# A 96-row pass taken apart: 64 rows of one half beside 32 rows of the other

## The chip, the cores and the metric

The kernel runs on one core of a Trainium2 chip. The metric is device time in microseconds of one execution, as the median of several runs. The core has a matrix engine (TensorE, PE in the profile, with its weight loads as PEld), a vector engine (VectorE, DVE), a scalar engine (ScalarE, ACT), GpSimd (POOL) and SyncE (SP), which issues most DMA transfers. Each engine works through its own instructions in order; engines wait for each other by semaphores.

## The reference

Two branches over an input of 2048 tokens with 576 features are mixed by a gate per token:

```python
def _A_ref(x, w_r, w_i):
    X = jnp.fft.rfft2(x, axes=(-2, -1)) * (w_r + 1j * w_i)
    return jnp.fft.irfft2(X, s=(S, D), axes=(-2, -1))

def _B_ref(x, w_gate, w_up, w_down):          # w_gate, w_up: 576 x 4608, w_down: 4608 x 576
    h = _gelu(x @ w_gate) * (x @ w_up)
    return h @ w_down

g = _sigmoid((A_x * gate_w).sum(-1, keepdims=True))
return g * _A_ref(A_x, w_r, w_i) + (1 - g) * _B_ref(B_x, w_gate, w_up, w_down)
```

## The kernel before

The float32 operands are split in a high and a low part, and a product of two such operands is made of three TensorE passes: high times high, low times high, high times low. A *pass* here is one weight load with one matmul behind it.

The gate and up products (`x @ w_gate` and `x @ w_up`) take most of the passes. For most of the work they are computed by a scheme with seven products of half-sized blocks, as in Strassen's method, in place of eight. The class `Block` holds the weights' side. Its groups run over the token halves and over pairs of 128 hidden features, 34 groups in all; `products(b, k)` runs one group with the seven products named a11, a12, s2, s3, s1, a22 and s4 (n = 0 to 6). Each product is made for two halves s = 0 and 1 of 128 rows of output each (gate and up), and each half goes into a PSUM buffer of 128 x 512: `px` (two buffers, px0 and px1) and `pgu` (two buffers) take turns as `fore` and `acc`.

The contraction over a block of 288 features is two tiles of 128 rows and a rest of 32. For one half, `seven` issues six passes of 128 rows (L1324) and for the rest one pass of 96 rows (L1326): the three passes of high and low parts are stacked as 3 x 32 rows, so that one pass does them. The stacked rest of the weights is loaded into a slot by a DMA of SP (`tail` in `prep`, L1303, tensor `tails`), the stacked rest of the inputs is in `til` or `xtl`.

After products 0, 2 and 3 ScalarE copies each half's buffer (`copy`, L234): for n = 0 into the buffer of `acc` (`px<-pgu` or `pgu<-px`), for n = 2 and 3 into `xraw`. The buffers then go on being added to: product 1 adds to those of product 0, product 3 to those of product 2, product 5 to those of product 3. After products 4 and 6 VectorE adds the buffer to `xraw` (`add`, L1367). In the opening group (k = 0) the copies of products 0 and 2 are issued directly behind the seven passes, before anything else (`soon`).

Between the products stand steps of the down product (`down`, L927): twelve passes of 128 rows over 288 columns into the buffer `pdn`, copied out with a scale by ScalarE (L959, `stg`) and added in DRAM by a DMA of GpSimd (L940). An ordinary group has one such step behind each product and two behind the last; the opening group has none behind its first five.

The spectral branch (the Fourier transforms) runs beside this on VectorE, ScalarE and the DMA queues, with some passes on TensorE (L332). It is written as generators, and its place among the rest is set while the program is being built: each pass adds to a credit (`tick`), and at each `gap()` the branch issues work for as long as credit is left, which is capped at 2.0. `at(n, fn)` puts a function off by n gaps. `gap()` thus sets the order of instructions on every engine. Part of the branch's work are the column butterflies, with quarter turns on ScalarE (`turned`, L248 and L249) and additions on VectorE (L257, L262, L278), on tiles that DMAs bring from DRAM (`rows<-away`).

Of the kernel before, what the change touches and what calls it, by code (L numbers as in the profile page):

```python
# [15 lines left out]
P = 128  # L16
# [143 lines left out]
def _build(nc, tc, a):  # L160
    with ExitStack() as ctx:
# [3 lines left out]
        vec, act, pl, pe = nc.vector, nc.scalar, nc.gpsimd, nc.tensor  # L165
# [4 lines left out]
        def f(x):  # L170
            return x.bitcast(F32)
# [52 lines left out]
        def ps_x(c):  # L224
            return psum.tile([P, TB], F32, name=f"px{c}", tag=f"px{c}", bufs=1)
# [7 lines left out]
        def copy(o, i):  # L233
            act.activation(o, i, AF.Copy)  # L234
# [497 lines left out]
        def tick(us):  # L732
            credit[0] += rate[0] * us

        def at(n, fn):

            if n == 0:
                fn()
                return
            later.append((count[0] + n, fn))  # L740
            later.sort(key=lambda x: x[0])

        def gap():

            count[0] += 1
            while later and later[0][0] <= count[0]:
                later.pop(0)[1]()
            if aux:
                aux.pop(0)()
            credit[0] = min(credit[0], cap[0])  # L750
            if not gens:
                return
            while credit[0] > 0:
                try:
                    v = next(gens[0])
                except StopIteration:
                    gens.pop(0)
                    v = None
                if v is None:
                    while side and credit[0] > 0:  # L760
                        v = next(side[0], None)
                        if v is None:
                            break
                        credit[0] -= v
                    return
                credit[0] -= v
# [42 lines left out]
        def seq(key, *steps):  # L809

            q = todo[key] = [fn for _, fn in steps]
            for n, _ in steps:
                at(n, lambda: q and q.pop(0)())

        def due(key):
            q = todo.pop(key, [])
            while q:
                q.pop(0)()
# [86 lines left out]
        def split_h(g, hold, wants=(), soon=False):  # L905

            def high():
                hold.append(take(wants))
                copy(hold[0][:, 0], g)

            def low():
                vec.tensor_tensor(hold[0][:, 1], g, f(hold[0][:, 0]), ALU.subtract)
                credit[0] -= 0.7

            return ((1, high), (2, low)) if soon else ((3, high), (5, low))
# [93 lines left out]
        ops = {}  # L1009
# [216 lines left out]
        class Block:  # L1226
# [87 lines left out]
                c, d = (2, 4)  # L1314
                seq(("b", k, m), (lead, total), (lead + c, high), (lead + c, tail), (lead + d, rest_of))

            def seven(self, ps, k, m, x, s, first, soon=None):

                due(("b", k, m))
                w, (xh, xl, xt) = self.slot(k, m), ops[x]  # L1320
                for t in range(2):
                    hi, lo = (w[:, n + P * s:n + P * (s + 1)] for n in ((256, 0), (768, 1024))[t])
                    for q, (l, x) in enumerate(((hi, xh), (lo, xh), (hi, xl))):
                        pe.matmul(ps, l, x[:, t], start=first and t == 0 and q == 0, stop=False,  # L1324
                                  skip_group_check=True)
                pe.matmul(ps, w[0:96, 512 + P * s:512 + P * (s + 1)], xt[0:96], start=False, stop=True,  # L1326
                          skip_group_check=True)
                tick(7 * 0.2265)
                if soon:
                    soon()  # L1330
                gap()

        def products(b, k):

            p, i = b.groups[k]
            j = p * NT + 2 * i
            u, u3 = ([xraw[:, 2 * q + s] for s in range(2)] for q in range(2))
            made = {}
            opening, end, turn = k == 0, k == len(b.groups) - 1, (p, i) == (0, NBLK - 1)
            if 0 < k < len(PAIRS):  # L1340
                for q in range(2):
                    for n, fn in zip((1, 6, 7, 9, 10), tail_piece(2 * k + q)):
                        at(n + 11 * q, fn)

            def finish(name, x, o):
                g, v = x
                hold = made[name] = []

                def mult():
                    vec.tensor_tensor(o, o, v, ALU.mult)  # L1350
                    credit[0] -= 0.69

                def gelu():
                    act.activation(o, g, AF.Gelu_apprx_tanh)

                wants = dict(c21=extra[1:], c22=extra[:1]).get(name, base)
                if end and name in ("c21", "c12"):
                    gelu()
                    seq((name, k), (1, mult), *split_h(o, hold, wants, True))
                else:  # L1360
                    soon = 0 if end else 1
                    high, low = (fn for _, fn in split_h(o, hold, wants))
                    late = name in ("c22", "c12") and not end
                    seq((name, k), (1 + late, gelu), (2 + (soon if name != "c21" else 0) + late, mult), (4 + soon + late - end, high), (5 + 2 * soon + late, low))

            def add(o, v):
                vec.tensor_tensor(o, o, v, ALU.add)  # L1367
                credit[0] -= 0.69

            fore, acc = ([f() for f in fs] for fs in ((ps_gu, ps_gu), (lambda: ps_x(0), lambda: ps_x(1)))[::1 - 2 * (k % 2)])  # L1370
            downs = (0, 0, 0, 0, 0, 1, 1) if opening else (2, 2, 2, 2, 2, 0, 0) if end else (1, 1, 1, 1, 1, 1, 2)
            for n, (name, nd) in enumerate(zip(("a11", "a12", "s2", "s3", "s1", "a22", "s4"), downs)):
                m = n + 3
                b.prep(k + m // 7, m % 7)
                if n == 0 and k:
                    b.load_d(k)
                if n == 4:
                    w, x = dns[:, j % 4:j % 4 + 2], b.both
                    copy(w[:, :, 0], x)

                    def rest_of(w=w, x=x):
                        vec.tensor_tensor(w[:, :, 1], x, f(w[:, :, 0]), ALU.subtract)
                        credit[0] -= 1.35

                    seq(("dn", j), (5, rest_of))
                if n == 3 and opening:
                    b.more()
                if n == 0:
                    b.load(k + 1, "r11", "r21")
                elif n == 3:  # L1390
                    b.load(k + 1, "r22")
                elif n == 4:
                    b.load(k + 1, "r12")
                if n == 4:
                    fore = [ps_x(s) for s in range(2)] if k % 2 else [ps_gu() for _ in range(2)]
                ps = acc if n in (2, 3, 5) else fore
                for s in range(2):
                    soon = opening and n in (0, 2)
                    b.seven(ps[s], k, n, name, s, n in (0, 4), (lambda n=n, s=s: copy((acc, None, u)[n][s], ps[s])) if soon else None)
                    if n in (0, 2, 3) and not soon:  # L1400
                        copy((acc, None, u, u3)[n][s], ps[s])
                    elif n in (4, 6):
                        at(0 if end else 1, lambda x=(u3, u)[n // 2 - 2][s], y=ps[s]: add(x, y))
                if turn and n == 1:
                    ops["hold"] = True
                if turn:
                    assert ops["kept"]
                    at(2, lambda name=name: swap(name))
                if n in (1, 4, 5, 6):
                    finish(*{1: ("c11", fore, gl[0]), 4: ("c22", u3, u3[0]), 5: ("c21", acc, gl[1]), 6: ("c12", u, u[0])}[n])  # L1410
                for _ in range(nd):
                    if pend:
                        down(*pend.pop(0))
                if end and n == 5:
                    while gens:
                        credit[0] = 1.0
                        gap()
                    load_last(1)
            if turn:
                at(1, lambda: ops.pop("hold"))  # L1420
            due(("dn", j))
            for tb, names in ((1, ("c21", "c22")), (0, ("c11", "c12"))):
                d = (p, i, tb, tuple((j + q, made[names[q]], (names[q], k)) for q in range(2)))
                pend.extend((d, t) for t in range(4))
# [46 lines left out]
        ps = ps_gu()  # L1471
# [87 lines left out]
        b = Block()  # L1559
# [72 lines left out]
```

## Time and profile before

| | |
|---|---|
| median of the two timed runs | 1417.51 us (1417.21 to 1417.8) |
| profiled execution | 1420.83 us, span 1419.1 us |
| mean granted TensorE clock | 0.968 |
| PE busy | 1334.9 us (94%), 7210 passes |
| DVE, ACT, POOL busy | 80%, 59%, 19% |
| DMA, mean over the span | 186 GB/s |

The span runs from the first to the last instruction of the profiled execution; the rest of its time lies around it. Busy time of TensorE counts the records of matmuls, which overlap, and whose ends are modelled: what a pass costs is read from the distance between starts. A wait is put down to the engine and line that ended it.

### The profile page before, as it was taken

The numbers are of one execution on the slowest core, as the hardware profiler recorded it, in microseconds if no ns is written. First come the engines' busy times: TensorE is split into PE (matmuls) and PEld (weight loads), VectorE is DVE, ScalarE is ACT, GpSimd is POOL, SyncE is SP. The second block draws the span as 40 slices with busy tenths as digits, with TensorE's granted clock in tenths as the row PEclk, the third lists the DMA queues.
The fourth block names the chain that finished last, engine by engine and source line by source line (L and its number), as shares of the span: only waits on it lengthen the run. The fifth ranks groups of instructions, "written<-read, shape, count | busy, mean of one in ns | idle before, by whom it ended". The sixth has DMA issues, their size and how long they took to land.

```text
span 1419.1 us, 20623 instructions
## 1 busy us (share of the span) xinstructions
PE 1334.9 (94%) x7210; PEld 1172.4 (83%) x7210; DVE 1140.0 (80%) x1750; ACT 842.2 (59%) x1419; POOL 273.3 (19%) x339
## 2 busy tenths in 40 slices
PE   9989789899999998899995986899999999999998
PEld 7878678788888887788884875788888888888888
DVE  7788677887999877687685766776899996999964
ACT  6565544467565656776664765766655557556552
POOL 0011111121111211122220121221211114111141
PEclk9999899899999999999997998999999999999999
DMA  9658788798676799989993784787877779877798
GB/s 346 184 121 178 176 184 182 155 259 182 133 134 133 132 304 295 245 179 268 325 228 88 209 210 105 145 197 144 213 131 135 137 131 231 168 136 138 134 207 219
DMA packets 169895, 263.33 MB, mean 186 GB/s; under 512 B 18688, under 2 KB 83520, under 8 KB 168768
## 3 DMA queue, kind: packets, MB, share of 16 engines
q0 software_dynamic: 47424, 91.51, 41.8%
q1 hardware_dynamic: 121936, 170.07, 37.8%
q8 instruction: 56, 0.92, 0.3%
q14 instruction: 47, 0.39, 0.1%
q10 hardware_dynamic: 432, 0.44, 0.1%
HBM read 141.23 MB, written 123.08 MB: 186 GB/s over the span
## 4 chain that ended last, share of the span: by engine, by line
PE 53%; ACT 4%; DVE 3%; DMA 2%; issue 1%; SPq 0%; DVEq 0%; ACTq 0%
PE pdn L927 19%; PE px L1324 14%; PE pgu L1324 14%; PE pgu L1326 2%; PE px L1326 2%; PE pdn L332 1%; DMA gub<-wf 1%; DMA rows<-away 1%; ACT low L248 1%; ACT low L249 1%; DVE rows L262 1%; ACT stg L959 0%; DVE rows L257 0%; ACT tmp L234 0%; DMA slot<-tails 0%
## 5 line engine op out<-in xcount | busy, mean ns | idle before, releaser
L940 POOL DMA_DIRECT2D yd<-stg x264 | 228.1, 867 | 1064.1 <-ACT stg L959 1004.0
L959 ACT ACTIVATE stg<-pdn,omg 128x576 f32<-128x576 f32 x276 | 204.6, 742 | 376.2 <-PE pdn L927 237.9
L927 PE MATMUL pdn<-dn,hb 128*128 128x288 f32 x1356 | 203.7, 298 | 5.0 <-ACT stg L959 5.0
L927 PEld LDWEIGHTS pdn<-dn,hb 128*128 128x128 f32 x1356 | 195.4, 191 | 14.1 <-ACT stg L959 6.0
L1324 PE MATMUL pgu<-til,gub 128*128 128x512 f32 x516 | 138.2, 404 | 33.7 <-ACT xraw L234 33.7
L1324 PE MATMUL pgu<-xhi,gub 128*128 128x512 f32 x480 | 152.2, 399 | 5.4 <-ACT px L234 4.0
L1324 PEld LDWEIGHTS pgu<-til,gub 128*128 128x128 f32 x516 | 97.7, 195 | 53.9 <-ACT xraw L234 34.6
L927 PE MATMUL pdn<-dn,ext 128*128 128x288 f32 x816 | 132.8, 299 | 9.2 <-ACT rows L234 9.2
L927 PEld LDWEIGHTS pdn<-dn,ext 128*128 128x128 f32 x816 | 124.6, 192 | 19.6 <-ACT rows L234 9.7
L927 PE MATMUL pdn<-dn,gub 128*128 128x288 f32 x816 | 130.9, 296 | 0.0
L927 PEld LDWEIGHTS pdn<-dn,gub 128*128 128x128 f32 x816 | 117.0, 191 | 0.0
L1311 DVE TENSOR_TENSOR gub<-low,gub 128x512 fp32r<-128x512 f32 x151 | 103.4, 685 | 16.7 <-ACT gub L234 16.7
L234 ACT ACTIVATE gub<-low 128x512 fp32r<-128x512 f32 (+1 forms) x163 | 100.7, 620 | 23.9 <-DVE low L1297 17.3
L1324 PE MATMUL px<-xhi,gub 128*128 128x512 f32 x344 | 110.1, 402 | 4.3 <-ACT pgu L234 4.3
L1324 PE MATMUL px<-til,gub 128*128 128x512 f32 x396 | 104.4, 400 | 9.0 <-ACT xraw L234 9.0
L1324 PEld LDWEIGHTS pgu<-xhi,gub 128*128 128x128 f32 x480 | 87.8, 190 | 21.6 <-ACT px L234 4.4
L1324 PE MATMUL pgu<-xlo,gub 128*128 128x512 f32 x240 | 94.2, 393 | 0.0
L1324 PEld LDWEIGHTS px<-til,gub 128*128 128x128 f32 x396 | 74.2, 192 | 24.1 <-ACT xraw L234 9.2
L1324 PEld LDWEIGHTS px<-xhi,gub 128*128 128x128 f32 x344 | 63.6, 193 | 15.8 <-ACT pgu L234 4.5
L1367 DVE TENSOR_TENSOR xraw<-xraw,px 128x512 f32<-128x512 f32 x68 | 45.6, 684 | 35.6 <-PE px L1326 35.4
L927 PE MATMUL pdn<-dn,hx 128*128 128x288 f32 x444 | 70.3, 294 | 0.0
L1326 PE MATMUL pgu<-til,gub 96*128 96x512 f32 x172 | 68.5, 398 | 0.0
(300 smaller groups left out, 2741.1 us busy)
## 6 DMA issues: line engine op xcount, KB each, us to landing
yd<-stg POOLq DMA_DIRECT2D x264, 288.0 KB, 5.0
low<-ws SPq DMA_DIRECT2D x114, 256.0 KB, 4.9
gub<-wd SPq DMA_DIRECT2D x68, 288.0 KB, 4.7
gub<-tails SPq DMA_DIRECT2D x179, 96.0 KB, 3.9
tails<-wtb SPq DMA_DIRECT2D x92, 112.0 KB, 3.5
slot<-tails SPq DMA_DIRECT2D x59, 96.0 KB, 4.1
gub<-ws SPq DMA_DIRECT2D x22, 256.0 KB, 5.0
rows<-away SPq DMA_DIRECT2D x32, 145.0 KB, 6.0
```

Source lines behind the costliest of these rows:

```text
L234: act.activation(o, i, AF.Copy)
L248: act.activation(o[0:64], x[64:128], AF.Copy, scale=-s)
L249: act.activation(o[64:128], x[0:64], AF.Copy, scale=s)
L262: vec.tensor_tensor(o, p, q, op)
L332: pe.matmul(v[:, al, :NK], cc[d][2 * al + q], two(x)[:, al], start=n == 0, stop=n == 2)
L927: pe.matmul(ps[half], h[:, l, c], d[:, q, half * HD:(half + 1) * HD], start=part == 0 and n == 0, stop=part == 1 and n == 2)
L940: pl.dma_start(yd[u], o, accum_op=ALU.add)
L959: at(n, lambda: put(u, lambda o: act.activation(o.rearrange("p (c k) -> p c k", c=2), v[:, :, 0:HD], AF.Copy, scale=omg[:, u:u + 1]), i == 0))
L1311: vec.tensor_tensor(v[:, 0:5:4], x, f(v[:, 1:4:2]), ALU.subtract)
L1324: pe.matmul(ps, l, x[:, t], start=first and t == 0 and q == 0, stop=False, skip_group_check=True)
L1326: pe.matmul(ps, w[0:96, 512 + P * s:512 + P * (s + 1)], xt[0:96], start=False, stop=True, skip_group_check=True)
L1367: vec.tensor_tensor(o, o, v, ALU.add)
```

## The change

`seven` now issues only the six passes of 128 rows for a half, and then a gap. When both halves have had theirs, a new function, `rest_of_seven`, issues the rest for both: four passes, of 64 rows (rows 0 to 63) for one half and 32 rows (rows 64 to 95) for the other, and then the same with the halves exchanged. The operands, and where they lie, are as before. The copies and additions that follow a half now stand behind the rest of both halves, and the special place of the opening group's copies is gone.

```diff
-            def seven(self, ps, k, m, x, s, first, soon=None):
+            def seven(self, ps, k, m, x, s, first):
...
-                pe.matmul(ps, w[0:96, 512 + P * s:512 + P * (s + 1)], xt[0:96], start=False, stop=True,
-                          skip_group_check=True)
-                tick(7 * 0.2265)
-                if soon:
-                    soon()
+                tick(6 * 0.2265)
                 gap()
+
+            def rest_of_seven(self, ps, k, m, x):
+
+                w, xt = self.slot(k, m), ops[x][2]
+                for n in range(2):
+                    for s, (lo, hi) in ((n, (0, 64)), (1 - n, (64, 96))):
+                        pe.matmul(ps[s], w[lo:hi, 512 + P * s:512 + P * (s + 1)], xt[lo:hi], start=False, stop=lo == (64, 0)[s],
+                                  skip_group_check=True)
+                tick(2 * 0.2265)
...
                 for s in range(2):
-                    soon = opening and n in (0, 2)
-                    b.seven(ps[s], k, n, name, s, n in (0, 4), (lambda n=n, s=s: copy((acc, None, u)[n][s], ps[s])) if soon else None)
-                    if n in (0, 2, 3) and not soon:
+                    b.seven(ps[s], k, n, name, s, n in (0, 4))
+                b.rest_of_seven(ps, k, n, name)
+                for s in range(2):
+                    if n in (0, 2, 3):
                         copy((acc, None, u, u3)[n][s], ps[s])
```

On TensorE, the first product of the first ordinary group (k = 1) stood like this; px0 and px1 are the buffers of the two halves, slot holds the weights.

```order
L1324 MATMUL px0_1027<-xhi0_63,slot_74 128x512 x2
L1324 MATMUL px0_1027<-xlo0_65,slot_74 128x512
L1324 MATMUL px0_1027<-xhi0_63,slot_74 128x512 x2
L1324 MATMUL px0_1027<-xlo0_65,slot_74 128x512
L1326 MATMUL px0_1027<-til0_302,slot_74 128x512
L1324 MATMUL px1_1028<-xhi0_63,slot_74 128x512 x2
L1324 MATMUL px1_1028<-xlo0_65,slot_74 128x512
L1324 MATMUL px1_1028<-xhi0_63,slot_74 128x512 x2
L1324 MATMUL px1_1028<-xlo0_65,slot_74 128x512
L1326 MATMUL px1_1028<-til0_302,slot_74 128x512
L927 MATMUL pdn_1062<-dn_75,hb2_79 128x288 x6
```

The same product in the changed kernel, in which the sizes are those of what is written:

```order
L1324 MATMUL px0_1041<-xhi0_63,slot_74 128x512 x2
L1324 MATMUL px0_1041<-xlo0_65,slot_74 128x512
L1324 MATMUL px0_1041<-xhi0_63,slot_74 128x512 x2
L1324 MATMUL px0_1041<-xlo0_65,slot_74 128x512
L1324 MATMUL px1_1042<-xhi0_63,slot_74 128x512 x2
L1324 MATMUL px1_1042<-xlo0_65,slot_74 128x512
L1324 MATMUL px1_1042<-xhi0_63,slot_74 128x512 x2
L1324 MATMUL px1_1042<-xlo0_65,slot_74 128x512
L1334 MATMUL px0_1041<-til0_302,slot_74 128x512
L1334 MATMUL px1_1042<-til0_302,slot_74 128x512 x2
L1334 MATMUL px0_1041<-til0_302,slot_74 128x512
L927 MATMUL pdn_1078<-dn_75,hb2_79 128x288 x6
```

The pass of half 0 that stood at L1326 between the halves is gone from there; four passes at L1334 stand behind both halves, ahead of the down step.

The second place is on ScalarE, where the profile of before has TensorE's longest wait, around 748 us. The first rows before, with the copy of half 0 (`xraw_83<-pgu_6432`) and the first of the branch's quarter turns:

```order
L234 ACTIVATE gub0_812<-pdn_6512 128x290
L234 ACTIVATE xraw_83<-pgu_6432 128x512
L234 ACTIVATE gub1_72<-low_76 128x2x256
L248 ACTIVATE low_76<-rows_94 64x580
L249 ACTIVATE low_76<-rows_94 64x580
```

Five such rows further on, the end of the branch's part, with the copy of half 1 (`xraw_83<-pgu_6433`) and the copy of a down step (L959) behind it:

```order
L249 ACTIVATE low_76<-rows_94 64x580
L234 ACTIVATE tmp_5046<-rows_94 128x580
L248 ACTIVATE wtb_88<-wtb_88 64x580
L249 ACTIVATE wtb_88<-wtb_88 64x580
L234 ACTIVATE xraw_83<-pgu_6433 128x512
L959 ACTIVATE stg0_84<-pdn_6595,omg_92 128x576
```

The same place in the changed kernel:

```order
L234 ACTIVATE gub0_812<-pdn_6771 128x290
L234 ACTIVATE gub1_72<-low_76 128x2x256
L234 ACTIVATE xraw_83<-pgu_6667 128x512
L234 ACTIVATE xraw_83<-pgu_6668 128x512
L959 ACTIVATE stg0_84<-pdn_6809,omg_92 128x576
L248 ACTIVATE low_76<-rows_94 64x580
L249 ACTIVATE low_76<-rows_94 64x580
```

Both halves' copies and the down step's copy now stand ahead of the branch's quarter turns. At the second longest wait, around 849 us, the order changes in the same way.

## The prediction

> **What bounds the kernel now.** I read the page first: the busy time of the engines, the slices, and the chain that ended last.
>
> ```profile
> span 1419.1 us, 20623 instructions
> PE 1334.9 (94%) x7210; PEld 1172.4 (83%) x7210; DVE 1140.0 (80%) x1750; ACT 842.2 (59%) x1419; POOL 273.3 (19%) x339
> ...
> PE   9989789899999998899995986899999999999998
> ...
> PE 53%; ACT 4%; DVE 3%; DMA 2%; issue 1%; SPq 0%; DVEq 0%; ACTq 0%
> ```
>
> TensorE is busy in 94% of the span and carries over half of the chain; no other engine has more than 4% of it. So a pass that takes longer on TensorE lengthens the kernel by as much, and what can be won beside that is the idle 84 us (1419.1 - 1334.9). Next I asked whom TensorE waited for, and what it did around the two longest waits; the columns of the second view are the stretch, its length, the busy time of each engine, and the granted clock.
>
> ```profile
> PE pgu L1324 <- ACT xraw L234: 33.7, 3, 15.8
> PE px L1324 <- ACT xraw L234: 17.1, 2, 9.0
> ...
> 740.00:764.00 24.00, 8.33 (x48) 7.08 (x46) 12.15 (x18) 11.73 (x20) 1.44 (x2) 0.75 0.47 116
> 764.00:779.50 15.50, 15.41 (x73) 13.56 (x74) 9.29 (x15) 6.89 (x12) 0.00 (x0) 0.83 0.36 112
> 848.00:863.00 15.00, 2.01 (x14) 1.70 (x12) 8.81 (x12) 8.08 (x13) 0.00 (x0) 0.72 0.30 67
> 863.00:878.50 15.50, 15.40 (x67) 13.01 (x68) 8.35 (x13) 8.02 (x14) 2.56 (x3) 0.83 0.56 107
> ```
>
> The idle time stands in a few lumps. The two largest leave TensorE idle for 24.00 - 8.33 = 15.7 us and 15.00 - 2.01 = 13.0 us, and after each the clock granted over the next 15.5 us is only 0.83. Both are waits for a ScalarE copy out of PSUM. They return below, because the change moves those copies.
>
> **The passes: what one costs.** The row counts the passes of 96 rows, and the timeline shows one among its neighbours (start, duration; PEld is the weight load that goes with each pass).
>
> ```profile
> 0.00:1419.10 1419.10, 188.64 (x476) 90.73 (x476) 0.97 0.80 186
> ...
> 300.55 0.19 PEld L1326 LDWEIGHTS px<-til,slot 96*128 96x128 f32 x1
> 300.77 0.39 PE L1326 MATMUL px<-til,slot 96*128 96x512 f32 x1
> 300.77 0.95 PEld L927 LDWEIGHTS pdn<-dn,ext 128*128 128x128 f32 x6
> 301.00 0.96 PE L927 MATMUL pdn<-dn,ext 128*128 128x288 f32 x6
> 301.67 0.85 PEld L927 LDWEIGHTS pdn<-dn,gub 128*128 128x128 f32 x6
> 301.80 0.95 PE L927 MATMUL pdn<-dn,gub 128*128 128x288 f32 x6
> 302.45 0.32 PEld L1324 LDWEIGHTS pgu<-xhi,gub 128*128 128x128 f32 x2
> 302.58 0.63 PE L1324 MATMUL pgu<-xhi,gub 128*128 128x512 f32 x2
> ```
>
> There are 476 such passes, two per product, so 238 products. A pass over 512 columns occupies TensorE for 301.00 - 300.77 = 0.23 us, though its record lasts 0.39: the next pass starts before the last one has drained. Passes over 288 columns follow at (301.80 - 301.00)/6 = 0.133 us. A weight load starts at the same moment as the pass ahead of it (300.77 and 300.77), and in no pass of the trace before it: loads run one pass ahead and no further. And a pass starts as little as 0.133 us after its own load did, so that this is the closest step at which the trace shows different weights taking their turn.
>
> The change takes out two passes of 0.23 us per product and puts in four: 64 rows for half 0, 32 rows for half 1, 64 rows for half 1, 32 rows for half 0. Streamed columns stay at 512 each. No short pass, and no two passes beside each other, stand in this trace, so the price per product is bounded:
>
> - From below, each 32-row pass lies wholly beside its 64-row pass: two steps of 0.23, extra 0. Less than that isn't to be had, since each half still needs rows 0 to 63 for one whole pass.
> - In between, passes on different rows run together but their weights come one after the other, as the loads above do. With the first short pass at 0, the second starts at 0.133; the third needs rows 0 to 63, free at 0.23, and its weights, at 0.267; the fourth starts at 0.40 (its rows are free at 0.363). The next full pass needs all rows: 0.40 + 0.23 = 0.63. Before it started at 0.46. Extra 0.17.
> - Strictly one after the other: 4 x 0.23 - 0.46 = 0.46 extra.
> - From above, each change of height lets the array drain, so that a pass is paid with its 0.39 and the full pass ahead with its last 0.16: 4 x 0.39 + 0.16 - 0.46 = 1.26 extra.
>
> I take the middle one, 0.17, since it is the only one that keeps both things the rows show, loads one ahead and a closest step of 0.133. Times 238: **+40.5 us**, with ends 0 and 300.
>
> Here a rule of the Trainium skill speaks for the lower end. The page "TensorE: Matmul & The Clock Gate", section "Part 3: Packing small matmuls — row/col tiling", says that matmuls on different row groups start some 4 ns apart; by it the sum of the passes would be an estimate of 238 x 2 x 0.004 = 2 us. The same section says that a weight load overlaps a running matmul only where the row group differs, which this trace contradicts: the loads at 300.77 and 301.00 run under passes on the same rows.
>
> **The copies.** After products 0, 2 and 3 of a group ScalarE copies each half out of PSUM, and the product that next adds to that buffer waits for it. Half 0 used to be copied under the seven passes of half 1; now both copies come behind the last short pass.
>
> ```profile
> 85.28 0.40 PE L1326 MATMUL pgu<-til,gub 96*128 96x512 f32 x1
> ...
> 85.71 0.58 ACT L234 ACTIVATE px<-pgu 128x512 f32<-128x512 f32 x1
> ...
> ACT xraw L234 <- PE pgu L1326: 20.3, 40, 1.4
> ACT xraw L234 <- PE px L1326: 19.3, 37, 2.2
> ```
>
> From the start of the last pass to the end of its copy is 85.71 + 0.58 - 85.28 = 1.0 us. In ordinary groups a down step of twelve passes, 12 x 0.133 = 1.6 us, lies between, and ScalarE stood waiting for the pass before 77 of 136 such copies: hidden, at nothing. If ScalarE were late by its usual other work (0.6 to 0.7 us) it would still nearly fit; without that cover 66 places would pay up to 1.0 - 0.23 = 0.8 us, 50 us in all. Only the opening group has no down step there: two places, 2 x 0.8 = **+1.6 us**. The loads of the tail weights on SP's queue wait for the last reader of a slot, which stands at the product's end as before; the loads behind it move only with TensorE.
>
> **The two long waits.** In program order ScalarE's copy stood behind quarter turns (L248) of the spectral branch's column butterflies, whose inputs a DMA brought late. Rows of ScalarE at both places:
>
> ```profile
> 750.10 0.69 ACT L248 ACTIVATE low<-rows 64x580 f32<-64x580 f32 x1 [4.74 <-DMA rows<-away]
> ...
> 763.44 0.60 ACT L234 ACTIVATE xraw<-pgu 128x512 f32<-128x512 f32 x1
> ...
> 849.14 0.69 ACT L248 ACTIVATE low<-rows 64x580 f32<-64x580 f32 x1 [2.69 <-DMA rows<-away]
> ...
> 862.45 0.60 ACT L234 ACTIVATE xraw<-pgu 128x512 f32<-128x512 f32 x1
> ```
>
> The order of the change has the branch some steps later at these places, and both halves' copies (and a copy for the down steps) ahead of the butterflies. TensorE can then do up to two more products and down steps, 8 to 10 us of passes, before the next copy behind the butterflies stops it: up to 18 us less in the two. Against it, where the branch's work is issued in the second gap of a product, both copies now stand behind it, which begins a wait one half earlier, 1.6 us; ten waits for such copies would make 16. What is late next is in the first case the copies of product 3, behind the same butterflies. I take **-8 us**, the larger of the two waits halved, out of -18 to +16.
>
> **The sum.** 40.5 + 1.6 - 8 = +34 us. The profiled execution took 1420.8 us with its span of 1419.1, which gives 1455; it stands 3.3 us above the median of the runs, 1417.5, so the forecast for the timed runs is **1452 us**, +2.4%.
>
> **Rivals.**
> 1. *The passes lie wholly beside each other*: 1417.5 + 1.6 - 8 = 1411. For it speaks that nothing but the weights joins the two rows' work; against it, that no load in the trace runs more than one pass ahead, though full passes can't show whether it might.
> 2. *The change doesn't do what it says*, and the four run one after the other: 238 x 0.46 = 110, so 1417.5 + 110 + 1.6 - 8 = 1521. For it: no two of 7210 passes run together in the trace, as none could.
> 3. *Drained only going in and out*: 0.16, then 0.23 for the first pair and 0.39 for the second, less 0.46, is 0.32; times 238 is 76, so 1487. Drained at every change of height: 300, so 1711. The trace has no change of height to speak for or against. A rule of the Trainium skill gives the last: "TensorEngine Tiling (Array Packing)", section "Tiling Modes", says that a change of tiling mode drains the engine, and 128, 64 and 32 rows are three modes there; no run here shows it yet.
> 4. *Faster*: the reordered copies free TensorE of both long waits while the passes cost nothing. Idle 15.7 + 13.0 us and two times 15.5 x (1 - 0.83) = 2.6 us at a reduced clock are 34 us: 1417.5 + 1.6 - 34 = 1385. It decides from the point where the copies of product 3 as well stand ahead of the butterflies; in the order they don't.
>
> **How the numbers follow.** Forecast 0.30, beside each other 0.29, one after the other 0.14, drained in and out 0.13, drained each time 0.07, faster 0.06, anything else 0.01. About 2%, 28 us, is what a measurement of this kernel can tell from no change, so same is 1389 to 1446. To it go rival 1 (0.29), a third of the forecast's own chance, whose range of 1435 to 1475 reaches below 1446 (0.10), and the rest (0.01): 0.40. Faster is rival 4, a little of which ends short: 0.05. Slower: 0.55. The range runs from 1398, rival 1 with most of the waits' gain, to 1530, rival 2 with the copies' waits unchanged; it leaves out rival 4 and the full drain, and fringes of the others, under 0.2. The likeliest case alone spans 1435 to 1475.
>
> **What would show it.** In the timeline of the changed kernel, the start of the second short pass after the first: near 0 for rival 1, 0.13 for the forecast, 0.23 or more for rival 2; and from the first short pass to the next full one 0.46, 0.63 or 0.92. The waits of TensorE for the copies at 748 and 850 us should have about halved in sum, and the opening group should show two waits under 1 us. The prediction is wrong if short passes cost by their rows instead of their columns, or if the branch, moved, meets its transfers at other places and makes new waits of ten microseconds.

## The result, and the profile after

The changed kernel takes 1691.04 us as the median of its runs (1688.97 to 1693.11) against 1417.51 us before: a ratio of 1.193, with a 95% interval of 1.1866 to 1.1993. The profiled execution has a span of 1691.0 us, 271.9 us more than before.

The page of the changed kernel, its span, the busy times, TensorE's slices and the chain that ended last:

```profile
span 1691.0 us, 21572 instructions
PE 1657.1 (98%) x7686; PEld 1224.8 (72%) x7686; DVE 1146.6 (68%) x1750; ACT 835.7 (49%) x1419; POOL 273.4 (16%) x339
PE   9999999999999999999997999999999999999999
PE 91%; ACT 3%; DMA 2%; DVE 2%; issue 1%; SPq 1%; DVEq 0%; ACTq 0%
PE pdn L927 27%; PE pgu L1324 18%; PE px L1324 18%; PE px L1334 11%; PE pgu L1334 11%; PE pdn L332 1%; DMA slot<-tails 1%; SPq L1221 1%; ACT stg L959 0%; PE px L863 0%; ACT low L248 0%; ACT low L249 0%; PE pgu L863 0%; DMA tmp<-xs 0%; DVE rows L262 0%
```

TensorE is now busy in 98% of a longer span, and 22% of that span is the new line, L1334, alone. The waits of TensorE in the changed kernel are fewer than before (engine and line, what it waited for, us in total, times, longest):

```profile
PE pgu L1324 <- ACT xraw L234: 13.7, 2, 10.4
PE pdn L927 <- ACT stg L959: 5.5, 4, 2.2
PE pdn L332 <- ACT stg L959: 4.3, 5, 0.9
PE px L1324 <- ACT xraw L234: 1.7, 2, 1.0
```

So the time went into passes, and some came back from waits. One product's rest in the timeline, weight loads first and then the passes:

```profile
1167.43 0.19 PEld L1324 LDWEIGHTS pgu<-xhi,gub 128*128 128x128 f32 x1
1167.66 0.19 PEld L1324 LDWEIGHTS pgu<-xlo,gub 128*128 128x128 f32 x1
1168.20 0.18 PEld L1334 LDWEIGHTS pgu<-xtl,gub 64*128 64x128 f32 x1 [0.35 <-issue]
1168.63 0.18 PEld L1334 LDWEIGHTS pgu<-xtl,gub 32*128 32x128 f32 x1 [0.25 <-issue]
1169.06 0.18 PEld L1334 LDWEIGHTS pgu<-xtl,gub 64*128 64x128 f32 x1 [0.25 <-issue]
1169.49 0.18 PEld L1334 LDWEIGHTS pgu<-xtl,gub 32*128 32x128 f32 x1 [0.25 <-issue]
1169.91 0.19 PEld L927 LDWEIGHTS pdn<-dn,hb 128*128 128x128 f32 x1 [0.24 <-issue]
```

```profile
1167.88 0.39 PE L1324 MATMUL pgu<-xlo,gub 128*128 128x512 f32 x1
1168.20 1.78 PE L1334 MATMUL pgu<-xtl,gub 64*128 64x512 f32 x4
1169.91 1.06 PE L927 MATMUL pdn<-dn,hb 128*128 128x288 f32 x6
1170.81 0.95 PE L927 MATMUL pdn<-dn,hx 128*128 128x288 f32 x6
```

Before, each load started with the pass ahead of it. Here the last full pass starts at 1167.88, and the first short pass's load only at 1168.20, together with its own pass; the next three loads follow at steps of 0.43 us, each with its pass, and so does the load of the next full pass at 1169.91. Here no pass runs beside another, and no weights are loaded ahead. From 1167.88 to 1169.91 are 2.03 us, where two passes of 96 rows took 3 x 0.23 = 0.69 from the last full pass to the next. One more 0.105 us follows: the six down passes from 1169.91 to 1170.81 take 0.90 us in place of 0.80. Together 1.34 + 0.105 = 1.445 us a product, and 238 products make 344 us. The span grew by 272. Of the other 72 us, 50 came back as idle time of TensorE, which fell from 1419.1 - 1334.9 = 84 us to 1691.0 - 1657.1 = 34. The rest is a remainder that wasn't measured by itself; it goes with the mean granted clock, which rose from 0.968 to 0.992, since the long waits were followed by stretches at a lower clock. Below, *waits* means both.

### The profile page after: what moved, and what is told of

Read it like the earlier page. It is cut to its first block, busy times and chain, and to the rows that moved or that the text cites. A ratio compares the mean times of both kernels' runs of the same rounds, so it can differ in the third digit from the quotient of the medians.

```text
span 1691.0 us, 21572 instructions
## 1 busy us (share of the span) xinstructions
PE 1657.1 (98%) x7686; PEld 1224.8 (72%) x7686; DVE 1146.6 (68%) x1750; ACT 835.7 (49%) x1419; POOL 273.4 (16%) x339
## 4 chain that ended last, share of the span: by engine, by line
PE 91%; ACT 3%; DMA 2%; DVE 2%; issue 1%; SPq 1%; DVEq 0%; ACTq 0%
PE pdn L927 27%; PE pgu L1324 18%; PE px L1324 18%; PE px L1334 11%; PE pgu L1334 11%; PE pdn L332 1%; DMA slot<-tails 1%; SPq L1221 1%; ACT stg L959 0%; PE px L863 0%; ACT low L248 0%; ACT low L249 0%; PE pgu L863 0%; DMA tmp<-xs 0%; DVE rows L262 0%
## 5 line engine op out<-in xcount | busy, mean ns | idle before, releaser
L959 ACT ACTIVATE stg<-pdn,omg 128x576 f32<-128x576 f32 x276 | 205.0, 743 | 550.9 <-PE pdn L927 291.4
L927 PE MATMUL pdn<-dn,hb 128*128 128x288 f32 x1356 | 213.3, 305 | 6.7 <-ACT stg L959 5.5
L927 PEld LDWEIGHTS pdn<-dn,hb 128*128 128x128 f32 x1356 | 186.2, 190 | 32.8 <-issue 23.4
L1324 PE MATMUL pgu<-xhi,gub 128*128 128x512 f32 x480 | 153.5, 402 | 14.8 <-ACT xraw L234 13.7
L1334 PE MATMUL pgu<-til,gub 64*128 64x512 f32 x344 | 153.6, 499 | 0.0
L927 PE MATMUL pdn<-dn,ext 128*128 128x288 f32 x816 | 143.7, 311 | 0.0
L927 PEld LDWEIGHTS pdn<-dn,ext 128*128 128x128 f32 x816 | 112.6, 188 | 31.3 <-issue 28.2
L1334 PEld LDWEIGHTS pgu<-til,gub 64*128 64x128 f32 x344 | 62.8, 182 | 95.0 <-issue 93.6
L1324 PE MATMUL pgu<-til,gub 128*128 128x512 f32 x516 | 125.4, 391 | 0.0
L1334 PE MATMUL px<-til,gub 64*128 64x512 f32 (+1 forms) x268 | 119.2, 497 | 0.0
L1311 DVE TENSOR_TENSOR gub<-low,gub 128x512 fp32r<-128x512 f32 x151 | 103.3, 684 | 13.7 <-ACT gub L234 13.7
L1334 PEld LDWEIGHTS px<-til,gub 64*128 64x128 f32 (+1 forms) x268 | 48.7, 182 | 72.4 <-issue 70.5
L1372 DVE TENSOR_TENSOR xraw<-xraw,pgu 128x512 f32<-128x512 f32 x68 | 43.7, 684 | 78.5 <-PE pgu L1334 78.5
```

The lines of the kernel that those rows point to most:

```text
L927: pe.matmul(ps[half], h[:, l, c], d[:, q, half * HD:(half + 1) * HD], start=part == 0 and n == 0, stop=part == 1 and n == 2)
L959: at(n, lambda: put(u, lambda o: act.activation(o.rearrange("p (c k) -> p c k", c=2), v[:, :, 0:HD], AF.Copy, scale=omg[:, u:u + 1]), i == 0))
L1311: vec.tensor_tensor(v[:, 0:5:4], x, f(v[:, 1:4:2]), ALU.subtract)
L1334: pe.matmul(ps[s], w[lo:hi, 512 + P * s:512 + P * (s + 1)], xt[lo:hi], start=False, stop=lo == (64, 0)[s], skip_group_check=True)
```

## The experiments

Two theories were put up after this result. **H**: a change of height (the 128, 64 or 32 rows of the array that a pass uses) makes TensorE empty itself first, and passes of one height on different rows do run beside each other. **S**: a short pass never runs beside another nor takes its weights ahead, whatever its neighbour.

**Short passes in order of height.** The four passes of the change, in another order:

```diff
-                for n in range(2):
-                    for s, (lo, hi) in ((n, (0, 64)), (1 - n, (64, 96))):
+                for lo, hi in ((0, 64), (64, 96)):
+                    for s in range(2):
```

> The four short passes of a product are put in order of height: 64 rows for half 0, 64 rows for half 1, then 32 and 32. Theory H (each change of height lets the array drain): one step of 0.32 us in, then 0.23 between the two of 64 rows, 0.43 to the first of 32, 0.23 between these, 0.42 out: 1.63 us from the last full pass to the next one in place of 2.03, so 238 x 0.40 = 95 us less than the change, some 1596 to 1610 us. Theory S (a short pass never takes its weights ahead, whatever its neighbour): 2.03 as before, 1691 us.

Measured: 1608.95 us, ratio to before 1.1362 (1.1342 to 1.1382), 82 us less than the change, as H has it. Its timeline, loads and passes:

```profile
1129.35 0.29 PEld L1334 LDWEIGHTS px<-til,gub 64*128 64x128 f32 x2 [0.35 <-issue]
1130.01 0.29 PEld L1334 LDWEIGHTS px<-til,gub 32*128 32x128 f32 x2 [0.36 <-issue]
1130.66 0.30 PEld L927 LDWEIGHTS pdn<-dn,hb 128*128 128x128 f32 x2 [0.36 <-issue]
```

```profile
1129.03 0.39 PE L1324 MATMUL px<-xlo,gub 128*128 128x512 f32 x1
1129.35 1.39 PE L1334 MATMUL px<-til,gub 64*128 64x512 f32 x4
1130.67 0.40 PE L927 MATMUL pdn<-dn,hb 128*128 128x288 f32 x1
```

The two loads of 64 rows now stand in one record of 0.29 us (0.18 for one): the second starts under the first pass, 0.11 us after it. From 1129.03 to 1130.67 are 1.64 us, against 1.63 forecast from H. S is out: a short pass takes its weights ahead when the pass in front has its own height.

**Two pairs of 64 rows.** The heights agree, and the halves lie on different rows:

```diff
+                xh = ops[x][0]
                 for n in range(2):
-                    for s, (lo, hi) in ((n, (0, 64)), (1 - n, (64, 96))):
-                        pe.matmul(ps[s], w[lo:hi, 512 + P * s:512 + P * (s + 1)], xt[lo:hi], ...
+                    pe.matmul(ps[0], w[0:64, 512 + P * n:512 + P * (n + 1)], xt[0:64], ...
+                    pe.matmul(ps[1], w[64:128, 256 + P * n:256 + P * (n + 1)], xh[64:128, 0], ...
```

> Four short passes per product as in the change, but all of 64 rows: rows 0 to 63 into the buffer of half 0 beside rows 64 to 127 into that of half 1, twice. It computes other sums (the lower rows are taken from other weights), only its time counts. Theory H: the two of a pair run beside each other, since their heights agree: 0.32 in, about 0 in the pair, 0.23, about 0, 0.42 out, 0.97 us from full pass to full pass in place of 2.03; 238 x 1.06 = 252 us less than the change, 1440 us, up to 1485 where the waits for ScalarE that the slower passes hid come back. If equal heights run without a drain but one after the other: 0.32 + 3 x 0.23 + 0.42 = 1.43, about 1550 us. Theory S: 1691 us.

Measured: 1495.37 us, ratio 1.0555 (1.0536 to 1.0575). Loads and passes of one product:

```profile
1043.36 0.18 PEld L1334 LDWEIGHTS px<-til,slot 64*128 64x128 f32 x1 [0.35 <-issue]
1043.36 0.18 PEld L1336 LDWEIGHTS px<-xhi,slot 64*128 64x128 f32 x1
1043.47 0.19 PEld L1334 LDWEIGHTS px<-til,slot 64*128 64x128 f32 x1
1043.47 0.19 PEld L1336 LDWEIGHTS px<-xhi,slot 64*128 64x128 f32 x1
1044.02 0.30 PEld L927 LDWEIGHTS pdn<-dn,ext 128*128 128x128 f32 x2 [0.36 <-issue]
```

```profile
1043.04 0.39 PE L1324 MATMUL px<-xlo,slot 128*128 128x512 f32 x1
1043.36 0.49 PE L1334 MATMUL px<-til,slot 64*128 64x512 f32 x1
1043.36 0.49 PE L1336 MATMUL px<-xhi,slot 64*128 64x512 f32 x1
1043.69 0.39 PE L1334 MATMUL px<-til,slot 64*128 64x512 f32 x1
1043.70 0.39 PE L1336 MATMUL px<-xhi,slot 64*128 64x512 f32 x1
1044.02 0.40 PE L927 MATMUL pdn<-dn,ext 128*128 128x288 f32 x1
```

The passes of a pair start within 0.01 us of each other, and their loads too. This is what the change was meant to get, and it got it nowhere. Two terms can be read off. Going from 128 rows to 64 takes 1043.36 - 1043.04 = 0.32 us instead of 0.23: 0.09 more, which fits an array that empties first (the emptying has no row of its own). And the first pass after a change of height starts together with its load, so that the next load begins 0.11 us later, and the next pass 1043.69 - 1043.36 = 0.33 us later instead of 0.23: 0.10 more. A change of height thus costs **some 0.2 us**, and a visit to another height two of them. From full pass to full pass it took 1044.02 - 1043.04 = 0.98 us, as expected (0.97), though the steps fall otherwise than I had them. The time was above my 1440 to 1485 because more waits came back than the 45 us allowed for: TensorE was idle for 1490.7 - 1422.4 = 68 us, 34 more than in the change, and the mean granted clock was 0.980, against 0.992.

**Two pairs of 32 rows** at the change's own places in the array:

```diff
-                    for s, (lo, hi) in ((n, (0, 64)), (1 - n, (64, 96))):
-                        pe.matmul(ps[s], w[lo:hi, 512 + P * s:512 + P * (s + 1)], xt[lo:hi], ...
+                    for s, lo in ((0, 0), (1, 64)):
+                        pe.matmul(ps[s], w[lo:lo + 32, 512 + P * n:512 + P * (n + 1)], xt[lo:lo + 32], ...
```

> Four short passes at the change's places in the array (rows from 0 for half 0, rows from 64 for half 1), but all of 32 rows, so that the heights agree. It leaves out the other rows of the rest. If unequal heights are what keeps the change's passes apart, pairs run beside each other as with two times 64 rows: 1495 us. If a pass of 32 rows can't run beside another, 0.23 to 0.43 us a pass and 1560 to 1691 us.

Measured: 1491.09 us, ratio 1.0527 (1.0498 to 1.0555), as with 64 rows. The four passes of one product stand in one record:

```profile
1042.71 0.73 PE L1334 MATMUL px<-til,slot 32*128 32x512 f32 x4
```

It lasts as long as the two pairs of 64 rows did, from 1043.36 to 1043.70 + 0.39. So neither the place nor 32 rows as such keeps the change's passes apart, only that their heights differ.

**One pair of 64 rows.** The second pair is left out:

```diff
-                for n in range(2):
...
+                xh = ops[x][0]
+                pe.matmul(ps[0], w[0:64, 512:512 + P], xt[0:64], ...
+                pe.matmul(ps[1], w[64:128, 256 + P:256 + 2 * P], xh[64:128, 0], ...
```

> One pair of 64 rows per product (rows 0 to 63 for half 0, rows 64 to 127 for half 1), in place of two pairs; it leaves out half of the rest and takes other rows for half 1. If a visit to another height costs a fixed price in and out, this is the run with two pairs less one step of 0.33 us: 1495 - 238 x 0.33 = 1416, up to 1440 as waits come back. If the price hangs on each short pass, half of what two pairs added to the move alone: 1431.6 + 32 = 1464.

Measured: 1457.95 us, ratio 1.0291 (1.0261 to 1.0322): 37 us less than two pairs, between the two expectations. My first one took away a step of 0.33 us, but 0.10 of that belongs to the visit and stays: 238 x 0.23 = 55, less what the waits take back. Even one pair, which has half the streaming time of two passes of 96 rows, is slower than these, at 1431.59 us in the same place (the move alone, below): what it saves, 0.23 us, is less than a visit's two changes.

**Four passes at full height.** As many passes as in the change, without a change of height:

```diff
-                    for s, (lo, hi) in ((n, (0, 64)), (1 - n, (64, 96))):
-                        pe.matmul(ps[s], w[lo:hi, 512 + P * s:512 + P * (s + 1)], xt[lo:hi], ...
+                    for s in (n, 1 - n):
+                        pe.matmul(ps[s], w[0:96, 512 + P * s:512 + P * (s + 1)], xt[0:96], ...
```

> Four passes per product as in the change, but each of 96 rows, which the program places at full height (128): halves 0, 1, 1, 0. The rest is thus added twice; only the time counts. If the changes of height are what costs in the change, this pays for the number of passes alone: two more of 0.23 us, 238 x 0.46 = 110 us over the move alone (1431.6), 1541 us, down to 1515 where slower passes hide waits. If four passes in a row with weights of their own are the cost, whatever their height, about 1691 us as in the change.

Measured: 1505.91 us, ratio 1.0625 (1.0596 to 1.0653); a little below the range, since waits were hidden again. The change makes as many passes at the same points of the program and takes 185 us more. That is the five changes of height of a product: 185 / 238 / 5 = 0.16 us each, after what the waits gave back.

**The move alone.** The rest of both halves stays two passes of 96 rows, but stands where the change puts it:

```diff
-                for n in range(2):
-                    for s, (lo, hi) in ((n, (0, 64)), (1 - n, (64, 96))):
-                        pe.matmul(ps[s], w[lo:hi, 512 + P * s:512 + P * (s + 1)], xt[lo:hi], ...
+                for s in range(2):
+                    pe.matmul(ps[s], w[0:96, 512 + P * s:512 + P * (s + 1)], xt[0:96], ...
```

> The move alone: the rest of both halves stands behind both, with the copies behind it, but as two passes of 96 rows. No short pass, so H and S agree on the passes: 0.46 us per product as before. If the waits of TensorE for ScalarE's copies fell from 84 us idle to 34 because the copies moved ahead of the branch's butterflies, about 1400 us or somewhat less (the two longest waits 8 to 18 us shorter); if they fell because slower passes gave the branch more time, 1417 to 1421 (1.6 us for the opening group).

Measured: 1431.59 us, ratio 1.0105 (1.0087 to 1.0123): 1% slower, where I had expected 1400 to 1421. The moved copies are not where the shorter waits come from as a whole. The two longest waits did become shorter; first before, then here:

```profile
764.09 0.80 PE L1324 MATMUL pgu<-til,gub 128*128 128x512 f32 x1 [15.76 <-ACT xraw L234]
863.10 0.79 PE L1324 MATMUL pgu<-til,gub 128*128 128x512 f32 x1 [13.09 <-ACT xraw L234]
```

```profile
783.67 0.80 PE L1324 MATMUL pgu<-xhi,gub 128*128 128x512 f32 x1 [13.73 <-ACT xraw L234]
879.34 0.80 PE L1324 MATMUL pgu<-xhi,gub 128*128 128x512 f32 x1 [8.75 <-ACT xraw L234]
```

That is 28.9 us before and 22.5 here. But all of TensorE's idle time rose from 84 to 1430.1 - 1337.7 = 92 us, so other waits grew by more.

**The split alone.** Passes of 64 and 32 rows at each half's old place, in the code of before:

```diff
-                pe.matmul(ps, w[0:96, 512 + P * s:512 + P * (s + 1)], xt[0:96], start=False, stop=True,
-                          skip_group_check=True)
+                for lo, hi in ((0, 64), (64, 96)):
+                    pe.matmul(ps, w[lo:hi, 512 + P * s:512 + P * (s + 1)], xt[lo:hi], start=False, stop=lo == 64,
+                              skip_group_check=True)
```

> The split alone: each half's 96-row pass becomes a pass of 64 rows and one of 32 at its old place, with the copies where they were. Per half H and S both give 0.32 in, 0.43, 0.42 out: 1.17 us in place of 0.46, so 476 x 0.71 = 338 us more than before. If slower passes alone make the waits for ScalarE shorter by some 47 us, as in the change, 1709 us; if it took the moved copies, 1755 us.

Measured: 1739.94 us, ratio 1.229 (1.2264 to 1.2315). That lies between my two numbers. The sum lacked the 0.10 us after the change back to 128 rows (it has the others in its steps of 0.43 and 0.42), and more waits went than the 47 us allowed for: 476 halves with three changes of 0.2 us and two passes in place of one are 476 x 0.83 = 395 us, and the span grew by 1737.7 - 1419.1 = 319, so 76 us of waits went. Its page:

```profile
span 1737.7 us, 21575 instructions
PE 1708.1 (98%) x7686; PEld 1205.0 (69%) x7686; DVE 1155.5 (66%) x1750; ACT 844.3 (49%) x1419; POOL 271.2 (16%) x339
```

Idle are 1737.7 - 1708.1 = 30 us, as few as in the change, and the copies stand where they always stood. Slower passes alone make most of the waits vanish. Compared with the change there is one change of height more per product, 238 x 0.2 = 48 us; the two differ by 49.

**Where the move's 14 us come from.** Two kernels, first the move with a higher cap on the branch's credit, then the kernel before with nothing but the copies moved:

```diff
-        cap = [2.0]
+        cap = [2.5]
```

> The move alone, as measured before at 1431.6 us, with the cap on the branch's credit raised from 2.0 to 2.5, so that the two passes of the rest and the twelve of a down step (credit 0.49 + 1.70) are no longer cut off in one gap. If the 14 us of the move come from the branch falling behind by the lost credit, about 1417 us; if they come from both copies standing behind both halves, about 1431 us still.

```diff
                 for s in range(2):
-                    soon = opening and n in (0, 2)
-                    b.seven(ps[s], k, n, name, s, n in (0, 4), (lambda n=n, s=s: copy(...)) if soon else None)
-                    if n in (0, 2, 3) and not soon:
+                    b.seven(ps[s], k, n, name, s, n in (0, 4))
+                for s in range(2):
+                    if n in (0, 2, 3):
                         copy((acc, None, u, u3)[n][s], ps[s])
```

> The kernel before with its 96-row passes and gaps in their old places, and only the copies of both halves moved behind the second half (in the opening group too). If the copies' place is what costs the 14 us of the move, about 1431 us; if the gaps and the credit are, 1417 to 1419 us (1.6 us for the opening group).

Measured: 1425.86 us, ratio 1.0075 (1.0048 to 1.0101), with the higher cap, and 1431.06 us, ratio 1.011 (1.0084 to 1.0135), with the copies alone. The copies' place alone costs all of it; whether the cap gives a third back isn't settled, since its interval overlaps that of the move. TensorE's waits with only the copies moved:

```profile
PE pgu L1324 <- ACT xraw L234: 33.0, 4, 15.6
PE px L1324 <- ACT xraw L234: 18.9, 6, 8.2
PE pgu L1324 <- ACT px L234: 14.1, 7, 5.5
PE pdn L927 <- ACT rows L234: 6.5, 2, 3.3
PE px L1324 <- ACT pgu L234: 6.0, 3, 5.5
```

The two long kinds are about as they were (33.7 and 17.1 before). What grew most is the third, for the copies after product 0, which before was:

```profile
PE pgu L1324 <- ACT px L234: 5.3, 4, 4.0
```

And most of the loss has a place, the stage that holds all quarter turns of the column butterflies. ScalarE is busy there in 344.07 of 530.00 us, 65%, against 59% over the whole span. The same stretch of work with only the copies moved, and before:

```profile
480.00:1020.00 540.00, 481.93 (x2588) 422.59 (x2586) 385.16 (x613) 343.12 (x580) 104.20 (x139) 0.95 0.83 208
```

```profile
480.00:1010.00 530.00, 478.06 (x2582) 420.58 (x2581) 383.90 (x609) 344.07 (x580) 104.66 (x139) 0.95 0.83 211
```

2588 and 2582 passes are the same work within 2 us, and it takes 10 us longer, which is most of the span's 1430.0 - 1419.1 = 11.

**A try at the waits themselves**, in the kernel before:

```diff
-                    yield from waits(4)
+                    yield from waits(8)
...
-                for n, fn in zip((1, 6, 7, 9, 10), tail_piece(2 * k + q)):
+                for n, fn in zip((1, 8, 9, 10, 11), tail_piece(2 * k + q)):
```

> The kernel before with two numbers changed that give the branch's transfers more gaps: 8 in place of 4 between the load of four column tiles and their use, and the tail weights' sums and what follows one or two gaps later. If TensorE's waits come from transfers that get too few gaps, as the vanished waits behind slower passes suggest, 1390 to 1410 us; if the branch merely falls behind and is caught up later, 1415 to 1425.

Measured: 1415.5 us, ratio 0.9994 (0.9977 to 1.0011): no difference. But its waits are not those of before:

```profile
PE pgu L1326 <- DMA gub<-tails: 7.7, 1, 7.7
PE px L1326 <- DMA gub<-tails: 7.5, 1, 7.5
PE px L1326 <- DMA slot<-tails: 4.2, 1, 4.2
```

Before, TensorE waited for copies to `xraw` at 167, 210 and 255 us, 9.0 + 4.8 + 8.1 = 21.9 us. Here it waits at 166, 212 and 254 us for tail weights, 19.4 us; the second edit, which makes the tail weights later, is the likely reason. The two longest waits hardly changed, 14.6 and 12.7 us. So the run doesn't show what more gaps would bring where the tail weights stay in time, and which transfer or step of the branch sets the length of the two longest waits isn't settled. No version here beats the kernel before.

The runs by what they contain, with 0.2 us for a change of height and 0.23 us for each step of a pass beyond the two of before:

| rest of a product | changes of height | steps | sum, us over before | measured, us over before |
|---|---|---|---|---|
| two of 96 rows, moved | 0 | 2 | 0 | 14 |
| four of 96 rows | 0 | 4 | 109 | 89 |
| one pair of 64 | 2 | 1 | 40 | 41 |
| two pairs of 64 | 2 | 2 | 95 | 78 |
| two pairs of 32 | 2 | 2 | 95 | 74 |
| 64, 64, 32, 32 | 3 | 4 | 252 | 192 |
| the change | 5 | 4 | 347 | 274 |
| 64, 32 at each half's place | 6 | 4 | 395 | 323 |

The sums run ahead of the measurements the more, the slower the passes are: 17 to 21 us at 100, 60 to 73 from 250 on. The waits go the same way: TensorE is idle for 92 us in the move, 81 with one pair, 66 to 72 with two pairs or four whole passes, 44 in the order of height, 34 in the change and 30 in the last row. The 14 us of the moved copies are in no sum.

## Why the prediction was wrong

**What bounds the kernel** was read rightly: passes cost what they cost, and the waits stood where the lumps were.

**The passes: the step that failed** is "I take the middle one, 0.17". It was 1.44 us. The second short pass started 0.43 us after the first, where this step has 0.13, and the next full pass 1169.91 - 1168.20 = 1.71 us after the first short one, where it has 0.63. The middle value was built of steps between passes of one height, and no row of the trace held a pass of another. Both things it kept, loads one ahead and a closest step of 0.133, hold only while the height stays. The mechanism that was left with a chance of 0.07, a drain at each change of height, is the one that runs. The rule of the Trainium skill that I named beside it ("TensorEngine Tiling (Array Packing)", section "Tiling Modes") is borne out by the steps of 0.43 us. It says nothing of loads that no longer run ahead, which the rows show as well. On a change of height it was the only evidence that there was, and it spoke against the change; I weighed it below a figure made from rows that didn't bear on it.

**The upper end was too low.** 1.26 us took the drain to be what a record lasts beyond the step, 0.39 - 0.23 = 0.16, and left out that the first pass after a change has no weights waiting. What the runs leave for a drain by itself is smaller, 0.09 us, and the late load costs about the same again. The likeness of 300 us to the 274 measured is luck: the passes cost 344.

**The lower end** has its rule too. The page of the Trainium skill "TensorE: Matmul & The Clock Gate", section "Part 3: Packing small matmuls — row/col tiling", lets passes on different row groups start some 4 ns apart, and the pairs of equal height do start within 0.01 us. It doesn't say that heights must agree.

**The copies** were priced at nothing in ordinary groups, with the down step as cover. The prediction named a ScalarE that is late, and put nothing for it. The runs show 14 us for the move and 15 for the copies alone, most of it in the stage of the butterflies. This fits a cover of 1.6 us that is enough elsewhere and too short there, where half 0's copy needed the seven passes of half 1 as well; that is a reading of the place, not shown by a run of its own.

**The two long waits**, -8 us by the new order on ScalarE: about right for these two, and wrong as the whole. In the move alone they are 6.4 us shorter, 28.9 - 22.5, but other waits grew by more, which the sum left out. In the changed kernel two waits of this kind are left, 13.7 us together. With the split alone and the copies at their old place two are left as well, 18.5 us, so most of that came from the slower passes. What the changed kernel saved on waits in all, some 72 us, came from passes slow enough to hide them, a term that the sum didn't have at all.

## What to carry to other kernels

Count the changes of height, not the rows: short passes can pay only if those of one height stand together, on different rows and, as in the runs here, into different PSUM buffers, and if a visit saves more than its two changes, 0.4 us or nearly two passes over 512 columns here; no run here had one that did. When a change brings an operation that the trace doesn't hold, numbers from rows of another kind don't bound it, and a documented rule against it deserves the larger chance. When the bounding engine gets slower, its waits for others shrink, so a measured loss understates what the passes cost; and a copy's slack is to be checked in the stage where its engine is fullest.

## What the hardware showed beyond that

Passes of equal height on different rows start within 0.01 us of each other, their loads too, with 64 rows and with 32. A change of height shows as two terms: the next pass starts 0.32 us after a pass whose weights had been loaded ahead, instead of 0.23, and its load starts with it instead of one pass ahead, which costs the pass after it 0.10 us. Where each pass has another height than the last, the two fall together and the step is 0.43 us.
